# A speech joint network's gradients on one core: three loads and products moved in order, and another end of the program

## The chip, the cores and the metric

The kernel runs on one core of one Trainium2 chip. The core has five engines that each work through a list of instructions of their own: TensorE (PE, matrix products, with its weight loads PEld), VectorE (DVE), ScalarE (ACT), GpSimd (POOL) and SyncE (SP), which here only issues transfers. Transfers are issued by SP (which makes the hardware queue's requests) and by POOL (the software queue's), and run on the core's 16 DMA engines. An instruction whose input is not there holds up everything behind it in its engine's list. The metric is the time of one execution on the device in microseconds (us), lower is better; the time of a kernel is the median of its timed runs.

## The reference

The kernel computes a forward pass and all its gradients, in bfloat16. Cut to what matters:

```python
B, T, D, K, U = 2, 16000, 256, 3, 8
h  = gelu(conv(x, w1))[:, ::2]          # 3 taps, every second row kept: 8000 rows per batch
f  = gelu(conv(h, w2))[:, ::2]          # again: 4000 rows per batch
fe = f @ w_f;  ge = g @ w_g             # g: 8 prompts per batch, "bud,de->bue"
j  = tanh(fe[:, :, None, :] + ge[:, None, :, :])   # 2 x 4000 x 8 x 256
out = j @ w_o
# returned: out, and the gradients of x, w1, w2, g, w_f, w_g, w_o for a given grad_out
```

So the outputs are out_0 (the joint's product), out_1 (gradient of x), out_2 and out_3 (of w1 and w2, 3 x 256 x 256 each), out_4 (of the prompts g), out_5, out_6 and out_7 (of w_f, w_g and w_o, 256 x 256 each). The gradients of the weights are sums over all rows.

## The kernel before

The 2 x 4000 rows of the joint (with 16 empty ones between the batches) are one long line that is cut into G = 16 blocks of 512 columns; the last, block 15, has 336. The main loop over n does, in stage n, the joint of block n in four steps (`up` = 0 to 3, two prompts each) and, between its pieces, the convolutions of block n + 1 and the whole backward pass of block n - 1. `weave` mixes the two by a ratio written by hand. After the loop, the backward pass of block 15 stands alone.

**One step of the joint** (`joint_units`). `gj` (L653 to L667) multiplies the turned gradient GOT by w_o (L661, PE) and forms NGZ (L665, DVE); POOL adds the eight NGZ of a block up (L684) to NGFE. `o_block` makes out_0 (L710 on PE, L712 on ACT), which POOL stores (L737). `gwo` (L749) adds to w_o's gradient with rows JR of the tanh and rows GO of the gradient, one step later than they are loaded.

**Transfers.** SP issues, in one list, the turning loads of x (XC, L162) and of the gradient (GOT, L174), the plain loads of the gradient (GO, L204), the turning of the tanh into rows (JR, L691, in `load_jr`) and of F = gelu(conv) into rows (FR, L497, in `load_fr`, called when `up` is 1). POOL issues the stores of out_0 (L737) and of x's gradient (L257, in `store_gx`) and the loads of x rows for w1's gradient: XR (L215, in `load_xr`) and, for block 14, three early pieces (L246, in `load_xr_early`, called in steps 2 and 3 of stage 14) into three XC buffers, two pieces of 512 KB and one of 64 KB. Besides, POOL clears the tails of the short last block, among them FT's (L364, in `conv2_units`); FT has two buffers, so block 15's is free when block 13's has been read, and its last reader is the transfer FR of block 13.

**Backward pass of a block.** `d1_units` (L454, needs NGFE), `row_units` (turns rows on PE, L490, copied out at L492), `d5_units` (L477, L480), `gwf_units` (w_f's gradient, L535), `gw2_units` (w2's, L553), `ghr_units` (more rows), `e_units`: for each of 4 sets (3 in block 15) x's gradient (`gx_block`, L616 on PE, L619 on ACT, two GX buffers) and, for the first three, one tap of w1's gradient (`gw1`, L629). The sums over blocks are kept by `flush` (L438, DVE) in the fp32 tiles ACCF, ACC2 and ACC1.

**What sets the order.** The framework plans: it runs through the instructions with estimated times and gives each engine a list, in which an instruction that it takes to be ready can go ahead of others that were written earlier. Two means hold it back: `keep_in_program_order` (behind what was written before on the same engine) and `add_manual_dep` with NOSYNC (behind one named instruction of the same engine; an order, not a wait). `load_xr` has the first, `load_xr_early` and `load_fr` have none. `late` and `later` hold GELU pieces that `pump` hands out between matmuls.

**Start.** While the first x arrives, `warm` runs products of zeros on PE (L799): 12, then the prompts' transposes of `prompt_units` (L807, they need GR8, loaded by POOL), then 9, then the convolution of block 0 (L336). The prompts' second unit (L816, GE) follows it.

**End.** After the last backward pass each fp32 sum is copied to a bf16 tile and stored by SP (ACC1 on ACT, L915; ACC2 on DVE, L918; ACCF, L921; w_o's sum from PSUM, L924), and the prompts' gradients are formed: a sum over NGGEc (L928), and per batch a product with w_g turned (L937, out_4), transposes (L943, L945) and a product with the prompts (L947), at last L951 and the store of out_6 (L952).

Of the kernel before, what the change touches and what calls it, by code (L numbers as in the profile page):

```python
# [32 lines left out]
def kernel(  # L33
# [206 lines left out]
    def load_xr_early(n, piece):  # L240
# [5 lines left out]
        nc.gpsimd.dma_start(out=t[:, :(r1 - r0) * D], in_=x_rows(x, b, row + r0, P, r1 - r0, 4 * nsets(n)))  # L246
# [3 lines left out]
    def store_gx(n, k, t):  # L250
        s = nsets(n)
        for b, q, col, w in segs(n):
            p0, p1, row = col // s, (col + w) // s, 4 * (q + k) - 3
            if q + k == 0:
                nc.gpsimd.dma_start(out=out_1[b, 0:1, :], in_=t[p0:p0 + 1, 3, :])
                p0, row = p0 + 1, row + 4 * s
            nc.gpsimd.dma_start(out=x_rows(out_1, b, row, p1 - p0, 4, 4 * s),  # L257
                                in_=t[p0:p1].rearrange("p f d -> p (f d)"))
# [175 lines left out]
    def flush(key, acc, ps):  # L434
        if first_flush[key]:
            nc.vector.tensor_copy(out=acc, in_=ps)
        else:
            nc.vector.tensor_tensor(out=acc, in0=acc, in1=ps, op=ALU.add)  # L438
# [55 lines left out]
    def load_fr(n):  # L494
        W = geom(n)[1]
        FR = packed(frp.tile([P, KT, 4, P], BF16, name="FR")[:], "k a d", n, k=KT, d=P)
        nc.sync.dma_start_transpose(out=FR.rearrange("p k a d -> p (k a) d"),  # L497
                                    in_=S[n]["FT"].rearrange("p k w -> p (k w)"))
        S[n]["FR"] = FR
# [28 lines left out]
    def gwf_units(n):  # L528
# [9 lines left out]
        flush("F", ACCF[:], ps[:])  # L538
# [3 lines left out]
    def gw2_units(n):  # L542
        W = geom(n)[1]
        HG = S[n]["HG"]
        for i in (1, 2, 0):
# [10 lines left out]
            flush("2", ACC2[:, i, :], ps[:])  # L556
# [39 lines left out]
    def e_units(n):  # L596
# [26 lines left out]
        def gw1(i):  # L623
# [10 lines left out]
            flush("1", ACC1[:, i, :], ps[:])  # L634
# [209 lines left out]
    for _ in chain(warm(12), islice(prompts, 1), warm(9), conv_units(0), prompts, islice(conv1, 2), islice(turned, 3),  # L844
                   conv2_units(0)):
        pass
# [7 lines left out]
    for n in range(G):  # L854
# [16 lines left out]
        for up in range(U // 2):  # L871
# [5 lines left out]
            if up == 1:  # L877
# [30 lines left out]
    for _ in chain(d1_units(n), alternate(row_units(n), d5_units(n)), gwf_units(n), gw2_units(n), ghr_units(n), e_units(n)):  # L908
        pass


    fin = gel
    for i in range(KK):
        t_ = fin.tile([P, 512], BF16, name="g_sq", tag="g_sq")
        nc.scalar.copy(out=t_[:], in_=ACC1[:, i, :])  # L915
        nc.sync.dma_start(out=out_2[i].rearrange("(dt p) n -> p dt n", p=P), in_=t_[:].rearrange("p (k n) -> p k n", k=KT))
        t_ = fin.tile([P, 512], BF16, name="g_s", tag="g_s")
        nc.vector.tensor_copy(out=t_[:], in_=ACC2[:, i, :])  # L918
        nc.sync.dma_start(out=out_3[i].rearrange("(dt p) n -> p dt n", p=P), in_=t_[:].rearrange("p (k n) -> p k n", k=KT))
    t_ = fin.tile([P, 512], BF16, name="g_x", tag="g_x")  # L920
    nc.vector.tensor_scalar(out=t_[:], in0=ACCF[:], scalar1=-1.0, scalar2=None, op0=ALU.mult)  # L921
    nc.sync.dma_start(out=out_5.rearrange("(dt p) n -> p dt n", p=P), in_=t_[:].rearrange("p (k n) -> p k n", k=KT))
    t_ = fin.tile([P, 512], BF16, name="g_x", tag="g_x")
# [3 lines left out]
    NGGE = accp.tile([P, KT, CW], FP32, name="ACCN")[:, 0, :B * KT * U].rearrange("p (b k u) -> p b k u", b=B, k=KT)  # L927
    nc.vector.tensor_reduce(out=NGGE.rearrange("p b k u -> p (b k u)"),  # L928
                            in_=NGGEc[:].rearrange("p b k u c -> p (b k u) c"),
                            axis=mybir.AxisListType.X, op=ALU.add)  # L930
    NGGEb = ngzp.tile([P, KT, CW], BF16, name="NGZ")[:, 0, :B * KT * U].rearrange("p (b k u) -> p b k u", b=B, k=KT)
    nc.vector.tensor_copy(out=NGGEb, in_=NGGE)
    GWG_ps = ps_f32()
    for b in range(B):
        gg = ps_f32()
        for kt in range(KT):
            nc.tensor.matmul(gg[:U, 0:D], lhsT=NGGEb[:, b, kt, :], rhs=WGT[:, kt, :], start=(kt == 0), stop=(kt == KT - 1))  # L937
# [45 lines left out]
```

## Time and profile before

| | |
|---|---|
| median of 3 timed runs | 838.62 us (830.61 to 847.44) |
| the profiled execution | 823.52 us |
| its span, first to last instruction | 821.7 us |
| mean granted TensorE clock | 0.998 |
| PE busy | 794.8 us, 97% of the span |
| ACT, DVE, POOL busy | 679.0, 619.3, 401.2 us |
| PE busy in a typical 50 us (200 to 250) | 49.73 us |
| PE busy in the first 60 us | 47.47 us |
| DMA, mean | 230 GB/s, the 16 engines' share at 9 tenths or more up to the last two slices of 40 |

How to read it: busy time is the time an engine spent in its instructions; a matmul's end is modelled, so that PE's busy time can hide short gaps. In a timeline row the columns are the start, the length, the engine, the line, the operation, what it writes and reads, how many instructions are merged, and in brackets the idle time of that engine before it with what ended it. "SPq" rows are the queue's own: their length is the time until SP had handed the transfer over, which includes waiting. The profiled execution is shorter than each of the three timed runs; durations below come from it.

### The profile page before, as it was taken

The numbers are of one execution on the slowest core, as the hardware profiler recorded it, in microseconds if no ns is written. First come the engines' busy times: TensorE is split into PE (matmuls) and PEld (weight loads), VectorE is DVE, ScalarE is ACT, GpSimd is POOL, SyncE is SP. The second block draws the span as 40 slices with busy tenths as digits, with TensorE's granted clock in tenths as the row PEclk, the third lists the DMA queues.
The fourth block names the chain that finished last, engine by engine and source line by source line (L and its number), as shares of the span: only waits on it lengthen the run. The fifth ranks groups of instructions, "written<-read, shape, count | busy, mean of one in ns | idle before, by whom it ended". The sixth has DMA issues, their size and how long they took to land.

```text
span 821.7 us, 16450 instructions
## 1 busy us (share of the span) xinstructions
PE 794.8 (97%) x6234; PEld 592.1 (72%) x6309; DVE 619.3 (75%) x1193; ACT 679.0 (83%) x1080; POOL 401.2 (49%) x422
## 2 busy tenths in 40 slices
PE   8778999999999999999999999999999999999997
PEld 3445867867777776877868678677777768678796
DVE  4996786977869788687876869778697886868534
ACT  4999897996979879798897979969798797788644
POOL 1265554553554445454586544535544454455641
PEclk9999999999999999999999999999999999999999
DMA  9999999999999999999999999999999999999963
GB/s 223 210 203 233 231 250 254 246 273 218 243 247 220 265 236 201 241 291 218 245 230 251 218 238 244 246 217 253 248 233 231 250 251 154 225 223 267 254 146 92
DMA packets 401383, 189.38 MB, mean 230 GB/s; under 512 B 349304, under 2 KB 385056, under 8 KB 401304
## 3 DMA queue, kind: packets, MB, share of 16 engines
q1 hardware_dynamic: 380984, 121.21, 81.5%
q0 software_dynamic: 20320, 67.12, 26.8%
q8 instruction: 49, 0.80, 0.5%
q14 instruction: 30, 0.25, 0.1%
HBM read 51.39 MB, written 50.34 MB: 124 GB/s over the span
## 4 chain that ended last, share of the span: by engine, by line
PE 83%; ACT 6%; DVE 5%; DMA 3%; issue 3%; POOL 1%; POOLq 0%; DVEq 0%; ACTq 0%
PE GWO_ps L749 12%; PE ps L710 12%; PE ps L661 10%; PE ps L616 9%; PE ps L629 9%; PE ps L336 7%; PE pst L490 5%; PE ps L553 5%; PE ps L477 5%; PE ps L371 4%; ACT JT L424 2%; PE ps L535 2%; PE ps L454 1%; DMA JR<-JT 1%; ACT OUT L712 1%
## 5 line engine op out<-in xcount | busy, mean ns | idle before, releaser
L684 POOL TENSOR_TENSOR ACCN<-ACCN,NGZ 128x1024 f32<-128x1024 f32 (+1 forms) x80 | 169.5, 2118 | 74.6 <-DVE NGZ L665 73.5
L665 DVE SCALAR_TENSOR_TENSOR NGZ<-JSQ,ps 128x512 bf16<-128x512 bf16 (+3 forms) x272 | 168.4, 640 | 46.6 <-PE ps L661 34.6
L424 ACT ACTIVATE JT<-FE,GE 128x512 bf16<-128x512 f32 (+3 forms) x272 | 176.2, 711 | 0.5
L712 ACT CAST OUT<-ps 128x512 bf16<-128x512 f32 (+1 forms) x252 | 145.9, 595 | 36.3 <-PE ps L710 34.9
L653 ACT ACTIVATE JSQ<-JT 128x1024 bf16<-128x1024 bf16 (+1 forms) x128 | 134.8, 1059 | 35.8 <-DVE NGZ L665 35.6
L710 PE MATMUL ps<-WO,JT 128*128 128x256 bf16 (+1 forms) x1008 | 149.4, 272 | 4.9 <-DVE NGZ L665 3.8
L749 PE MATMUL GWO_ps<-GO,JR 128*128 128x256 bf16 (+1 forms) x1008 | 148.8, 273 | 2.8 <-DMA JR<-JT 2.1
L737 POOL DMA_DIRECT2D out_dram<-OUT x76 | 56.0, 738 | 165.2 <-ACT OUT L712 155.8
L661 PE MATMUL ps<-GOT,WOT 128*128 128x512 bf16 (+1 forms) x483 | 133.0, 374 | 2.4 <-ACT FE L397 0.9
L749 PEld LDWEIGHTS <-JR 128*128 128x128 bf16 (+1 forms) x1008 | 97.2, 98 | 29.7 <-DMA JR<-JT 3.6
L710 PEld LDWEIGHTS <-JT 128*128 128x128 bf16 (+1 forms) x1008 | 97.4, 98 | 26.3 <-issue 5.4
L616 PE MATMUL ps<-W1T,GH 128*128 128x256 bf16 (+2 forms) x756 | 100.4, 273 | 0.7
L616 PEld LDWEIGHTS <-GH 128*128 128x128 bf16 (+2 forms) x756 | 83.5, 116 | 13.0
L276 DVE SCALAR_TENSOR_TENSOR g_s<-g_sq,g_x 128x1024 bf16<-128x1024 bf16 (+2 forms) x35 | 67.9, 1940 | 30.3 <-ACT g_sq L276 30.3
L438 DVE TENSOR_TENSOR ACC<-ACC,ps 128x512 f32<-128x512 f32 x90 | 61.5, 684 | 36.9 <-PE ps L553 25.9
L336 PE MATMUL ps<-XC,W 128*128 128x512 bf16 (+1 forms) x359 | 85.2, 374 | 0.8
L629 PE MATMUL ps<-rows,XR 128*128 128x256 bf16 (+1 forms) x708 | 84.6, 273 | 0.0
L619 ACT CAST GX<-ps 128x512 bf16<-128x512 f32 (+2 forms) x126 | 72.4, 589 | 13.1 <-PE ps L616 5.8
L629 PEld LDWEIGHTS <-XR 128*128 128x128 bf16 (+1 forms) x708 | 69.3, 98 | 11.0
L257 POOL DMA_DIRECT2D out_dram<-GX x67 | 36.9, 551 | 81.2 <-ACT GX L619 79.4
L661 PEld LDWEIGHTS <-WOT 128*128 128x128 bf16 x512 | 48.2, 98 | 34.5 <-issue 3.5
L336 PEld LDWEIGHTS <-W 128*128 128x128 bf16 x384 | 37.5, 98 | 38.4 <-issue 0.4
(133 smaller groups left out, 1216.4 us busy)
## 6 DMA issues: line engine op xcount, KB each, us to landing
GO<-in_grad_out_dram SPq DMA_DIRECT2D x56, 512.0 KB, 5.5
out_dram<-OUT POOLq DMA_DIRECT2D x56, 512.0 KB, 5.9
out_dram<-GX POOLq DMA_DIRECT2D x55, 256.0 KB, 5.2
XR<-in_x_dram POOLq DMA_DIRECT2D x36, 256.0 KB, 9.3
XR<-in_x_dram POOLq DMA_DIRECT2D x12, 320.0 KB, 8.3
GO<-in_grad_out_dram SPq DMA_DIRECT2D x4, 384.0 KB, 5.0
out_dram<-OUT POOLq DMA_DIRECT2D x4, 384.0 KB, 5.0
GOT<-in_grad_out_dram SPq DMA_TRANSPOSE x68, 6.3
```

The lines of the kernel that those rows point to most:

```text
L336: nc.tensor.matmul(ps[:, :W], lhsT=W1[:, i, kt, mt * P:(mt + 1) * P], rhs=st["X", c][:, kt, 16 + sh:16 + sh + W], start=(k == 0), stop=(k ...
L424: act = nc.scalar.activation(out=JT[:, mt, lo:hi], in_=S[n]["FE"][:, mt, lo:hi], func=ACT.Tanh, bias=GE[:, b, mt, u:u + 1], scale=1.0)
L616: nc.tensor.matmul(ps[:M, cj * D:(cj + 1) * D], lhsT=GH[:, par, kt, o:o + s * (M - 1) + 1:s], rhs=W1T[:, i, kt, :], start=(j == 0), stop=( ...
L619: nc.scalar.copy(out=t[:M, 2 * cp:2 * cp + 2, :], in_=ps[:M, :])
L629: nc.tensor.matmul(ps[:, dt * D:(dt + 1) * D], lhsT=x_row(4 * k + i + 2 * (1 - par))[:M, dt * P:(dt + 1) * P], rhs=t[:M, g + 2 * par:g + 2 ...
L653: jsq = nc.scalar.activation(out=JSQ[:, :, :W], in_=JT[:, :, :W], func=ACT.Square)
L661: nc.tensor.matmul(ps[:, :W], lhsT=WOT[:, kt, mt * P:(mt + 1) * P], rhs=GOT[:, kt, :W], start=(kt == 0), stop=(kt == KT - 1))
L665: nc.vector.scalar_tensor_tensor(out=NGZ[:, mt, lo:hi], in0=JSQ[:, mt, lo:hi], scalar=1.0, in1=ps[:, lo:hi], op0=ALU.subtract, op1=ALU.mul ...
L684: st["last"] = nc.gpsimd.tensor_tensor(out=out, in0=in0, in1=st["NGZ", u][:, :, :W], op=ALU.add)
L710: nc.tensor.matmul(ps[:M, j * V:(j + 1) * V], lhsT=st["JT", u][:, kt, o:o + M], rhs=WO[:, kt, :], start=(kt == 0), stop=(kt == KT - 1))
L712: nc.scalar.copy(out=OUT[:M, k, :], in_=ps[:M, :])
L749: nc.tensor.matmul(GWO_ps[:, dt, :], lhsT=JR[:M, j, dt, k, :], rhs=GO[:M, k, j * V:(j + 1) * V], start=(n_gwo[0] == 0), stop=(n_gwo[0] == ...
```

## The change

The early x rows of block 14 are kept in program order on POOL. `load_fr` is called in step 3 of a stage instead of step 1, and from block 1 on the transfer stands behind the tanh rows JR of the block's last step. The two warm calls become one of 22, and both prompt units come behind the first convolution. In the last block `flush` writes the last sum straight into a bf16 tile (for w_f with the sign turned in the same instruction) and stores it; the prompts' gradients become a generator that alternates with w2's products; w_o's copy stands ahead of the last backward pass; and the last set's store of x's gradient is issued by SP.

```diff
@@ -243,7 +243,8 @@
         t = xcp.tile([P, 2, KT, CW + 16], BF16, name="XC")[:].rearrange("p c k w -> p (c k w)")
         (b, q, col, w), = segs(n)
         row = 4 * q - 3
-        nc.gpsimd.dma_start(out=t[:, :(r1 - r0) * D], in_=x_rows(x, b, row + r0, P, r1 - r0, 4 * nsets(n)))
+        tc.keep_in_program_order(nc.gpsimd.dma_start(out=t[:, :(r1 - r0) * D],
+                                                     in_=x_rows(x, b, row + r0, P, r1 - r0, 4 * nsets(n))))
         rows = t[:, :8 * D].rearrange("p (f d) -> p f d", f=8)
         S[n].setdefault("XRS", []).extend(rows[:, r] for r in range(r1 - r0))
 
@@ -254,8 +255,8 @@
             if q + k == 0:
                 nc.gpsimd.dma_start(out=out_1[b, 0:1, :], in_=t[p0:p0 + 1, 3, :])
                 p0, row = p0 + 1, row + 4 * s
-            nc.gpsimd.dma_start(out=x_rows(out_1, b, row, p1 - p0, 4, 4 * s),
-                                in_=t[p0:p1].rearrange("p f d -> p (f d)"))
+            queue = nc.sync if n == G - 1 and k == s - 1 else nc.gpsimd
+            queue.dma_start(out=x_rows(out_1, b, row, p1 - p0, 4, 4 * s), in_=t[p0:p1].rearrange("p f d -> p (f d)"))
             if q + w == MQ and k == 0:
                 nc.gpsimd.dma_start(out=out_1[b, T - 3:T, :].rearrange("(o f) d -> o f d", o=1), in_=t[p1:p1 + 1, 0:3, :])
 
@@ -431,8 +432,15 @@
 
     first_flush = {"1": True, "2": True, "F": True}
 
-    def flush(key, acc, ps):
-        if first_flush[key]:
+    def flush(key, acc, ps, to=None):
+        if to is not None:
+            o = gel.tile([P, 512], BF16, name="g_s", tag="g_s")
+            if key == "F":
+                nc.vector.scalar_tensor_tensor(out=o[:], in0=acc, scalar=-1.0, in1=ps, op0=ALU.mult, op1=ALU.subtract)
+            else:
+                nc.vector.tensor_tensor(out=o[:], in0=acc, in1=ps, op=ALU.add)
+            nc.sync.dma_start(out=to.rearrange("(dt p) n -> p dt n", p=P), in_=o[:].rearrange("p (k n) -> p k n", k=KT))
+        elif first_flush[key]:
             nc.vector.tensor_copy(out=acc, in_=ps)
         else:
             nc.vector.tensor_tensor(out=acc, in0=acc, in1=ps, op=ALU.add)
@@ -494,8 +502,10 @@
     def load_fr(n):
         W = geom(n)[1]
         FR = packed(frp.tile([P, KT, 4, P], BF16, name="FR")[:], "k a d", n, k=KT, d=P)
-        nc.sync.dma_start_transpose(out=FR.rearrange("p k a d -> p (k a) d"),
-                                    in_=S[n]["FT"].rearrange("p k w -> p (k w)"))
+        dma = nc.sync.dma_start_transpose(out=FR.rearrange("p k a d -> p (k a) d"),
+                                          in_=S[n]["FT"].rearrange("p k w -> p (k w)"))
+        if n:
+            tc.add_manual_dep(dma.ins, S[n]["JRD", 3].ins.name, NOSYNC, reason="rows of F behind tanh rows")
         S[n]["FR"] = FR
 
     def row_units(n):
@@ -535,7 +545,7 @@
                 nc.tensor.matmul(ps[:, dt * D:(dt + 1) * D], lhsT=FR[:M, dt, k, :],
                                  rhs=t[:M, 2 * k:2 * k + 2, :].rearrange("p k d -> p (k d)"),
                                  start=(k == 0 and dt == 0), stop=(k == len(bl) - 1 and dt == KT - 1))
-        flush("F", ACCF[:], ps[:])
+        flush("F", ACCF[:], ps[:], out_5 if n == G - 1 else None)
         first_flush["F"] = False
         yield
 
@@ -553,7 +563,7 @@
                     nc.tensor.matmul(ps[:, dt * D:(dt + 1) * D], lhsT=lhsT,
                                      rhs=HG[k][:M, 4:6, :].rearrange("p k d -> p (k d)"),
                                      start=(k == 0 and dt == 0), stop=(k == nsets(n) - 1 and dt == KT - 1))
-            flush("2", ACC2[:, i, :], ps[:])
+            flush("2", ACC2[:, i, :], ps[:], out_3[i] if n == G - 1 else None)
             yield
         first_flush["2"] = False
 
@@ -631,7 +641,7 @@
                                          rhs=t[:M, g + 2 * par:g + 2 * par + 2, :].rearrange("p k d -> p (k d)"),
                                          start=(j == 0 and dt == 0 and par == 0),
                                          stop=(j == len(bl) - 1 and dt == KT - 1 and par == 1))
-            flush("1", ACC1[:, i, :], ps[:])
+            flush("1", ACC1[:, i, :], ps[:], out_2[i] if n == G - 1 else None)
 
         for j, (k, M) in enumerate(bl):
             yield from gx_block(k, M)
@@ -841,7 +851,7 @@
     load_go(*orderp[0])
     load_got(*orderp[1])
     conv1, turned, prompts = conv_units(1), transposed_units(), prompt_units()
-    for _ in chain(warm(12), islice(prompts, 1), warm(9), conv_units(0), prompts, islice(conv1, 2), islice(turned, 3),
+    for _ in chain(warm(22), conv_units(0), prompts, islice(conv1, 2), islice(turned, 3),
                    conv2_units(0)):
         pass
     pump_late(len(late))
@@ -874,7 +884,7 @@
                 load_got(*orderp[step + 2])
             if step + 1 < len(orderp):
                 load_go(*orderp[step + 1])
-            if up == 1:
+            if up == 3:
                 load_fr(n)
             if back and up < 2 and n < G - 1:
                 load_xr(n - 1, 2 * up)
@@ -905,51 +915,45 @@
         gwo(*prev_gwo[0], k)
     for piece in range(4):
         load_xr(n, piece)
-    for _ in chain(d1_units(n), alternate(row_units(n), d5_units(n)), gwf_units(n), gw2_units(n), ghr_units(n), e_units(n)):
-        pass
-
-
-    fin = gel
-    for i in range(KK):
-        t_ = fin.tile([P, 512], BF16, name="g_sq", tag="g_sq")
-        nc.scalar.copy(out=t_[:], in_=ACC1[:, i, :])
-        nc.sync.dma_start(out=out_2[i].rearrange("(dt p) n -> p dt n", p=P), in_=t_[:].rearrange("p (k n) -> p k n", k=KT))
-        t_ = fin.tile([P, 512], BF16, name="g_s", tag="g_s")
-        nc.vector.tensor_copy(out=t_[:], in_=ACC2[:, i, :])
-        nc.sync.dma_start(out=out_3[i].rearrange("(dt p) n -> p dt n", p=P), in_=t_[:].rearrange("p (k n) -> p k n", k=KT))
-    t_ = fin.tile([P, 512], BF16, name="g_x", tag="g_x")
-    nc.vector.tensor_scalar(out=t_[:], in0=ACCF[:], scalar1=-1.0, scalar2=None, op0=ALU.mult)
-    nc.sync.dma_start(out=out_5.rearrange("(dt p) n -> p dt n", p=P), in_=t_[:].rearrange("p (k n) -> p k n", k=KT))
-    t_ = fin.tile([P, 512], BF16, name="g_x", tag="g_x")
+    t_ = gel.tile([P, 512], BF16, name="g_x", tag="g_x")
     nc.scalar.copy(out=t_[:], in_=GWO_ps[:].rearrange("p k v -> p (k v)"))
     nc.sync.dma_start(out=out_7.rearrange("(dt p) n -> p dt n", p=P), in_=t_[:].rearrange("p (k n) -> p k n", k=KT))
 
-    NGGE = accp.tile([P, KT, CW], FP32, name="ACCN")[:, 0, :B * KT * U].rearrange("p (b k u) -> p b k u", b=B, k=KT)
-    nc.vector.tensor_reduce(out=NGGE.rearrange("p b k u -> p (b k u)"),
-                            in_=NGGEc[:].rearrange("p b k u c -> p (b k u) c"),
-                            axis=mybir.AxisListType.X, op=ALU.add)
-    NGGEb = ngzp.tile([P, KT, CW], BF16, name="NGZ")[:, 0, :B * KT * U].rearrange("p (b k u) -> p b k u", b=B, k=KT)
-    nc.vector.tensor_copy(out=NGGEb, in_=NGGE)
-    GWG_ps = ps_f32()
-    for b in range(B):
-        gg = ps_f32()
-        for kt in range(KT):
-            nc.tensor.matmul(gg[:U, 0:D], lhsT=NGGEb[:, b, kt, :], rhs=WGT[:, kt, :], start=(kt == 0), stop=(kt == KT - 1))
-        gg_sb = rowp.tile([P, 8, P], BF16, name="rows")[:U, 0:2, :].rearrange("u a b -> u (a b)")
-        nc.scalar.activation(out=gg_sb, in_=gg[:U, 0:D], func=ACT.Copy, scale=-1.0)
-        nc.sync.dma_start(out=out_4[b], in_=gg_sb)
-        tr = ps_bf()
-        for kt in range(KT):
-            nc.tensor.transpose(out=tr[:U, kt, :], in_=NGGEb[:, b, kt, :], identity=ident[:])
-        ngR = rowp.tile([P, 8, P], BF16, name="rows")[:U, 0:KT, :]
-        nc.vector.tensor_copy(out=ngR, in_=tr[:U, 0:KT, :])
-        for dt in range(KT):
-            nc.tensor.matmul(GWG_ps[:, dt * D:(dt + 1) * D], lhsT=GRE[:, b, dt * P:(dt + 1) * P],
-                             rhs=ngR[:].rearrange("u kt p -> u (kt p)"),
-                             start=(b == 0 and dt == 0), stop=(b == B - 1 and dt == KT - 1))
-    t_ = fin.tile([P, 512], BF16, name="g_sq", tag="g_sq")
-    nc.scalar.activation(out=t_[:], in_=GWG_ps[:], func=ACT.Copy, scale=-1.0)
-    nc.sync.dma_start(out=out_6.rearrange("(dt p) n -> p dt n", p=P), in_=t_[:].rearrange("p (k n) -> p k n", k=KT))
+    def prompt_gradients():
+        NGGE = accp.tile([P, KT, CW], FP32, name="ACCN")[:, 0, :B * KT * U].rearrange("p (b k u) -> p b k u", b=B, k=KT)
+        nc.vector.tensor_reduce(out=NGGE.rearrange("p b k u -> p (b k u)"),
+                                in_=NGGEc[:].rearrange("p b k u c -> p (b k u) c"),
+                                axis=mybir.AxisListType.X, op=ALU.add)
+        NGGEb = ngzp.tile([P, KT, CW], BF16, name="NGZ")[:, 0, :B * KT * U].rearrange("p (b k u) -> p b k u", b=B, k=KT)
+        nc.vector.tensor_copy(out=NGGEb, in_=NGGE)
+        yield
+        gg, tr = ps_f32(), ps_bf()
+        for b in range(B):
+            for kt in range(KT):
+                nc.tensor.matmul(gg[:U, b * D:(b + 1) * D], lhsT=NGGEb[:, b, kt, :], rhs=WGT[:, kt, :],
+                                 start=(kt == 0), stop=(kt == KT - 1))
+            for kt in range(KT):
+                nc.tensor.transpose(out=tr[:U, b * KT + kt, :], in_=NGGEb[:, b, kt, :], identity=ident[:])
+        o = gel.tile([P, 512], BF16, name="g_sq", tag="g_sq")
+        nc.scalar.activation(out=o[:U], in_=gg[:U, 0:B * D], func=ACT.Copy, scale=-1.0)
+        nc.sync.dma_start(out=out_4.rearrange("b u d -> u b d"), in_=o[:U].rearrange("u (b d) -> u b d", b=B))
+        ngR = gel.tile([P, 512], BF16, name="g_sq", tag="g_sq")
+        nc.vector.tensor_copy(out=ngR[:U], in_=tr[:U, 0:B * KT, :].rearrange("u k p -> u (k p)"))
+        yield
+        ps = ps_f32()
+        for b in range(B):
+            for dt in range(KT):
+                nc.tensor.matmul(ps[:, dt * D:(dt + 1) * D], lhsT=GRE[:, b, dt * P:(dt + 1) * P],
+                                 rhs=ngR[:U, b * D:(b + 1) * D],
+                                 start=(b == 0 and dt == 0), stop=(b == B - 1 and dt == KT - 1))
+        o = gel.tile([P, 512], BF16, name="g_sq", tag="g_sq")
+        nc.scalar.activation(out=o[:], in_=ps[:], func=ACT.Copy, scale=-1.0)
+        nc.sync.dma_start(out=out_6.rearrange("(dt p) n -> p dt n", p=P), in_=o[:].rearrange("p (k n) -> p k n", k=KT))
+        yield
+
+    for _ in chain(d1_units(n), alternate(row_units(n), d5_units(n)), gwf_units(n),
+                   alternate(gw2_units(n), prompt_gradients()), ghr_units(n), e_units(n)):
+        pass
 
 
 # ---- launch: one core; inputs and outputs as the reference has them ----
```

## The prediction

> **What bounds the kernel now.** I read the page first: busy time by engine, then the chain that ended last.
>
> ```profile
> PE 794.8 (97%) x6234; PEld 592.1 (72%) x6309; DVE 619.3 (75%) x1193; ACT 679.0 (83%) x1080; POOL 401.2 (49%) x422
> ...
> PE 83%; ACT 6%; DVE 5%; DMA 3%; issue 3%; POOL 1%; POOLq 0%; DVEq 0%; ACTq 0%
> ```
>
> TensorE bounds it: of 821.7 us it leaves 26.9. The change adds and removes hardly any matmul, so it can only win from these. Busy times by stretch tell where they lie: in the first 60 us PE is busy 47.5 (12.5 lost); from 200 to 700, 50 us at a time, 49.7 (0.3 lost each, once 0.7); then
>
> ```profile
> 705.00:710.00 5.00, 4.95 (x44) 4.24 (x43) 4.93 (x12) 3.84 (x6) 2.59 (x5) 1.00 1.08 272
> 710.00:715.00 5.00, 4.04 (x28) 2.53 (x27) 3.49 (x5) 3.46 (x6) 4.80 (x4) 1.00 1.13 209
> 715.00:720.00 5.00, 4.12 (x27) 2.33 (x25) 2.08 (x5) 5.00 (x10) 2.96 (x4) 1.00 1.25 207
> ```
>
> (span, then busy PE, PEld, DVE, ACT, POOL, clock, DMA share, GB/s): 1.84 us lost, 1.7 more than the usual. From 760 to 765 it loses 1.02, and after its last large product, at 814.9, 6.8 us are left of the span. The rest is steady and out of reach.
>
> The timeline of the loss at 710, all engines:
>
> ```profile
> 688.10 10.91 SPq L174 DMA_TRANSPOSE GOT<-in_grad_out_dram  x1
> ...
> 700.91 2.70 SPq L497 DMA_TRANSPOSE FR<-FT  x1
> ...
> 704.33 3.62 SPq L691 DMA_TRANSPOSE JR<-JT  x1
> ...
> 705.74 0.23 POOL L364 MEMSET FT<- 128x96 bf16 x1 [10.29 <-issue]
> 706.26 0.55 POOL L257 DMA_DIRECT2D out_dram<-GX  x1 [0.29 <-ACT JT L424]
> ...
> 711.54 0.59 ACT L619 CAST GX<-ps 128x512 bf16<-128x512 f32 x1 [2.70 <-DMA out_dram<-GX]
> ...
> 712.18 1.02 PE L661 MATMUL ps<-GOT,WOT 128*128 128x512 bf16 x4 [0.83 <-ACT GX L619]
> ```
>
> POOL stands 10.29 us at L364: FT is not free until FR of block 13 has landed (issued 700.91, 4.4 median). Behind it stand GX's stores; ACT waits 2.70 for a GX buffer, PE 0.83 for ACT, and NGFE is late after that. FR was late because SP's list was: GOT took 10.91 where the same place a stage earlier took 3.24 (638.15). In just that time the first early load (POOL, issued 681.83, 512 KB) was under way, 16.1 us; from 680 to 690 the DMA engines moved 98 GB/s, a stage earlier (630 to 642) 307. That the load is the cause is my reading; the rate is low already from 680.0.
>
> **Part 1, early rows.** The first load, pinned behind block 14's store L737 of 737.42, goes to about 738, the others behind the store of 751.90. Issuing costs POOL 0.55 each: the pair fits in its idle 1.47 before L257 at 754.14; without that cover NGFE (760.39), for which PE already waits 0.97, is up to 1.1 later. The data are needed by w1's products at 784.3; 752.7 + 13.5 (median landing) = 766.2. Gain: SP's list at 690 to 704 is some 8 us earlier. The cost in stage 14 lies between 0 (the early load of 723.1, beside which PE was busy 19.88 of 720 to 740) and 8.6 (below). I take 0, by that row, the nearest. **Part 2, F's rows.** JR of each block's last step goes ahead of FR: by 1.24 to 3.07 us (FR's rows). JR of block 12 was issued at 646.24, landed 8.2 later and was used at 658.80: it has 4.4 us to spare, so the gain is 0 in this execution. FR's users have more: L535 of block 13 at 730.82, 25 us after landing; of block 15 at 803.29 against 784.4 + 2.5 + 1.2 + 4.4 = 792.5. For L364 it works against Part 1: 8 us earlier by the load, 3.6 (JR's 3.62) later by the order. Net 4.4 of the 10.29 us go, and I expect POOL's list, planned anew, to put L364 behind a store or an addition. What was late by at most 2.70 on ACT is then in time: **gain 1.7**, bounds 1.8 and, if L364 stays and FR is not earlier, a loss of 3.6. Next late is the loss at 760 (NGFE behind the 2.94 us clearing of XR), which stays.
>
> **Part 3, prompts.** The start:
>
> ```profile
> 1.82 5.18 PE L799 MATMUL ps<-rows 128*128 128x512 bf16 x12 [1.82 <-DVE rows L790]
> ...
> 7.93 0.25 PE L807 MATMUL pst<-ident,GX 8*128 8x8 bf16 x4 [0.93 <-DMA GX<-in_g_dram]
> 8.11 2.12 PE L799 MATMUL ps<-rows 128*128 128x512 bf16 x9
> ...
> 10.06 5.35 PE L336 MATMUL ps<-XC,W 128*128 128x512 bf16 x24
> ```
>
> Twelve warm products run at 0.427 us each (weight loads every 0.43), to 6.95; the next nine at (10.06 - 8.11)/9 = 0.217. Between them stands the wait for the prompts. Without it 22 end at 6.95 + 10 x 0.217 = 9.12, and the convolution starts 0.94 sooner. x is there: its second load was issued at about 2.2 and landed within 5.7, at 7.9; W1 at 1.3 + 5.0. Bounds: all 22 slow end at 11.2 (1.15 lost). The Trainium skill ("TensorE: Matmul & The Clock Gate", "What's actually happening") lets the clock rise after about 3.4 us of work, and says that the point varies by run; here the slow spacing still shows at 6.06, 4.2 us after the start, so the measurement decides. From 12.8 to 29 the chain runs through DVE, which takes on the copy gT, 0.17, that lay in its idle time; PE's wait for it is hidden, as PE waits for DVE there anyway (if not, 0.5). JR of step 0 follows the tanh, so all later moves along: **gain 0.94 - 0.2 = 0.7**.
>
> **Part 4, the end.** The chain, in order of time:
>
> ```profile
> 813.59 1.33 PE ps L629 x12
> 814.94 0.45 DVE ACC L438
> ...
> 817.13 0.39 PE ps L947 x2
> ...
> 817.59 0.60 ACT g_sq L951
> ```
>
> The last store was issued at 818.21 and took 1.8 to land. PE's list is full from 797 to 814.92 (6.00 of 6.00), so the prompts' products add to it there: 8 of 256 columns at 1.97/18 = 0.109 and 4 transposes at 0.06, 1.1 us, to 816.0. Then one flush of 0.69 to 816.7, no copy on ACT (0.62), and SP issues at 816.8: 818.21 - 816.8 = **1.4 sooner**. The last GX copy ends at 814.61 + 1.1 = 815.7; by SP, 0.4, and 1.8 to 3.0 to land (g_sq and g_x rows; POOL's 2.6): level with the last sum, so nothing more. The copies L915, L918, L921 (1.86, 1.08, 0.42) ran beside PE and give nothing; w_o's copy, 0.59, falls in ACT's idle 2.64 before 801.14. The sign in F's flush: 0.69, as the DVE rows of that form. Two waits are new. The prompts' last products wait for a copy on DVE (0 to 0.4). And the seven flushes share three g_s buffers: the fourth, w2's last at about 806.9, waits for F's store (804.9 + 0.4 + 2.1 = 807.4); behind it on DVE stand the row copies L492, for which PE's L629 waits. Bounds of the end: 0 and 1.5.
>
> **Sum.** 823.52 - 1.7 - 0.7 - 1.4 = 819.7, 3.8 us (0.46%) less. The three timed runs lie 7 to 24 above the profiled one, for a reason that the trace does not show; I take the same 3.8 from their median: 838.62 - 3.8 = **834.8**. Two per cent (16.8 us), about what three runs with this scatter tell from no change, is four times the forecast.
>
> **Rivals.** *A, slower: the early loads slow the end of stage 14.* GOT beside the first load landed 15.8 after issue instead of 6.3 (9.5 late), x 19.1 instead of 6.1 (13.0). In stage 14, JR of the last step (issued 752.27, 7.3 to land, used 765.76) has 6.2 to spare, GOT of step 1 (758.57 + 6.3, used 769.31) 4.4. Lateness beyond 4.4 is PE's; at 13.0 it is 8.6, more than the 3.8 won: 834.8 + 8.6 = 843.4. It turns to slower than before at 8.2 of lateness. For it: two loads of 512 KB, not one, 14 us apart. Against: the load of 723.1 cost PE nothing, and stage 14 turns no x (two transfers of 2.8). By the Trainium skill ("DMA: Bandwidth & Descriptors", "Queues, rings and completion order") an engine takes turns between its queues packet by packet; that would share the rate and not cut it to 98 GB/s, so by the rule alone, 512 KB at 290 GB/s, 1.8 us late, this rival would be nothing. Chance 0.15. *B, slower: the new order doesn't free POOL.* L364 stays where it was and FR, behind JR, is no earlier: POOL stands 3.6 longer, PE loses 3.6 instead of winning 1.7: 834.8 + 5.3 = 840.1. Chance 0.15. *C, faster by 2%:* what the timed runs have above the profile, 15.1 us, is JR coming too late at 14 boundaries (1.08 each, its 4.4 used up by a slower DMA); FR's place gives back 1.24 or more each, so all of it: 819.7. Nothing in the trace shows such waits after 68 us. Chance 0.08. *D, the clock rises sooner:* with 8 slow products (0.427) and 14 quick ones (0.217) the 22 end at 1.82 + 3.42 + 3.04 = 8.3, 0.8 sooner than in the sum: 834.0. Against it: the eleven slow spacings of the trace. The Trainium skill's 3.4 us, above, would be these 8 products. Chance 0.05. The forecast keeps 0.57.
>
> **Numbers.** Faster by over 2%: 0.09 (C, and scatter); slower by over 2%: 0.07 (A with more lateness, and scatter); within: 0.84. The range leaves out C and the upper edge of A: the runs' own scatter (-8.0, +8.8) about 834.8 is 826.8 to 843.6; widened by the unknown costs, 822 to 848.
>
> **What would show it.** Right: L364 with a short wait, PE 4.9 of 5 in 710 to 720's place; no L246 before stage 14's second store; L336 first at 9.1; JR ahead of FR at each boundary; the last SP issue 1.4 nearer to the last L629. Wrong: PE waiting for GOT or JR from 755 to 780, DVE waiting before its fourth g_s, slow spacing up to the 22nd warm product.

## The result, and the profile after

The changed kernel took 837.44 us, the median of 6 executions (829.5 to 855.1); the kernel before, beside it, 828.74 (824.61 to 847.44). The ratio is **1.0104, with a 95% interval of 1.0065 to 1.0143**: slower by 1.0%. (All ratios here leave out executions more than 1.5% above the fastest of their kernel, up to 7 of 12 where a kernel's times scatter most, so that there the median, which is over all executions, says more.) The forecast was 834.8 and 0.46% faster. The time lies within the 822 to 848 that was stated, but these are some 13 us to either side of a base, 838.62 from three executions, that was high: the 35 executions of the kernel before in the last comparison below have a median of 827.33. What counts is the ratio, and its sign was wrong.

The profiled execution of the changed kernel took 835.12 us, its span is 833.1, 11.4 longer than before's 821.7. The lines of the source have moved: FT's clearing is L365 (before L364), the stores of GX L259 (L257), the GX copies L629 (L619), NGFE L694 (L684), FR L505 (L497), JR L701 (L691), `gj`'s product L671 (L661), the large last products L639 (L629).

The page, busy time by engine and the chain that ended last:

```profile
PE 803.1 (96%) x6310; PEld 594.0 (71%) x6310; DVE 615.7 (74%) x1188; ACT 677.6 (81%) x1076; POOL 404.1 (48%) x421
...
PE 79%; ACT 7%; DMA 6%; DVE 3%; issue 2%; POOL 2%; SPq 0%; POOLq 0%; DVEq 0%; ACTq 0%
```

DMA has 6% of the chain instead of 3%. PE is busy 8.3 us longer, with no more work to speak of: some matmuls ran slower. Where, the stretches tell that answer to before's 705 to 720 (span, then busy PE, PEld, DVE, ACT, POOL, clock, DMA share, GB/s):

```profile
710.00:715.00 5.00, 5.00 (x44) 4.24 (x43) 4.93 (x12) 2.96 (x5) 0.00 (x0) 1.00 1.04 196
715.00:720.00 5.00, 1.31 (x12) 1.02 (x11) 0.01 (x1) 0.00 (x0) 2.86 (x5) 0.85 1.10 230
720.00:725.00 5.00, 0.50 (x2) 0.22 (x2) 0.00 (x0) 1.14 (x3) 3.40 (x2) 0.50 1.15 298
725.00:730.00 5.00, 5.00 (x20) 2.35 (x19) 2.08 (x6) 5.00 (x10) 1.42 (x3) 0.62 1.02 246
```

PE loses 8.2 us between 715 and 725, where before it lost 1.84 in all. Then it is "busy" for 5.00 us with 20 matmuls, where 44 fit from 710 to 715: the granted clock was 0.50 and 0.62. Three rows of the view of waits (us in total, times, longest) are one chain:

```profile
POOL FT L365 <- DMA FR<-FT: 15.0, 1, 15.0
...
ACT GX L629 <- DMA out_dram<-GX: 11.5, 2, 10.9
...
PE ps L671 <- ACT GX L629: 8.2, 1, 8.2
```

The timeline shows them in order:

```profile
699.85 0.56 POOL L259 DMA_DIRECT2D out_dram<-GX  x1
...
707.52 3.47 SPq L701 DMA_TRANSPOSE JR<-JT  x1
...
711.08 1.26 SPq L505 DMA_TRANSPOSE FR<-FT  x1
...
715.43 0.18 POOL L365 MEMSET FT<- 128x96 bf16 x1 [15.03 <-DMA FR<-FT]
715.96 0.54 POOL L259 DMA_DIRECT2D out_dram<-GX  x1 [0.35 <-issue]
...
723.86 0.58 ACT L629 CAST GX<-ps 128x512 bf16<-128x512 f32 x1 [10.90 <-DMA out_dram<-GX]
724.50 1.87 PE L671 MATMUL ps<-GOT,WOT 128*128 128x512 bf16 x4 [8.19 <-ACT GX L629]
```

FR of block 13 stands directly behind JR, as the change has it. The clearing stands in POOL's list where it stood before, with GX's store behind it, and waits 15.03 us for FR instead of 10.29. The store is issued at 715.96, and 7.8 later, by the chain that ended last, it sets ACT free; PE goes on when ACT has made its copy. Four matmuls that take 1.02 elsewhere take 1.87 after the stall.

The starts of NGFE, one per stage, show what this is of the 11.4 (after less before): +1.1 up to stage 7; up to stage 8 another 3.75 (from 423 to 453 the DMA engines moved 133 to 172 GB/s, before's 231 to 257; PE waits 1.8 there for XR rows, and the clock is 0.83 over the last ten us); then nothing until stage 12; from there to stage 14 **7.9** (4.8 and 3.1); stages 14 to 15 are equal, 31.52 in both; the end is 1.36 shorter. 1.1 + 3.75 + 7.9 - 1.36 = 11.4.

### The profile page after: what moved, and what is told of

It is laid out like the page before. It is cut to its first block, busy times and chain, and to the rows that moved or that the text cites. A ratio compares the mean times of both kernels' runs of the same rounds, so it can differ in the third digit from the quotient of the medians.

```text
span 833.1 us, 16510 instructions
## 1 busy us (share of the span) xinstructions
PE 803.1 (96%) x6310; PEld 594.0 (71%) x6310; DVE 615.7 (74%) x1188; ACT 677.6 (81%) x1076; POOL 404.1 (48%) x421
## 4 chain that ended last, share of the span: by engine, by line
PE 79%; ACT 7%; DMA 6%; DVE 3%; issue 2%; POOL 2%; SPq 0%; POOLq 0%; DVEq 0%; ACTq 0%
PE GWO_ps L759 11%; PE ps L720 11%; PE ps L671 10%; PE ps L639 9%; PE ps L626 9%; PE ps L337 7%; PE pst L498 5%; PE ps L563 5%; PE ps L485 4%; PE ps L372 4%; ACT JT L425 2%; DMA XR<-in_x_dram 2%; PE ps L545 2%; PE ps L462 1%; PE ps L396 1%
## 5 line engine op out<-in xcount | busy, mean ns | idle before, releaser
L694 POOL TENSOR_TENSOR ACCN<-ACCN,NGZ 128x1024 f32<-128x1024 f32 (+1 forms) x80 | 169.3, 2117 | 75.0 <-DVE NGZ L675 73.5
L671 PE MATMUL ps<-GOT,WOT 128*128 128x512 bf16 (+1 forms) x512 | 139.6, 377 | 8.5 <-ACT GX L629 8.2
L629 ACT CAST GX<-ps 128x512 bf16<-128x512 f32 (+2 forms) x126 | 72.4, 588 | 21.1 <-DMA out_dram<-GX 11.5
L337 PE MATMUL ps<-XC,W 128*128 128x512 bf16 (+1 forms) x360 | 87.3, 380 | 0.6 <-DMA XC<-in_x_dram 0.6
L639 PE MATMUL ps<-rows,XR 128*128 128x256 bf16 (+1 forms) x708 | 85.1, 273 | 1.8 <-DMA XR<-in_x_dram 1.8
L446 DVE TENSOR_TENSOR ACC<-ACC,ps 128x512 f32<-128x512 f32 x84 | 57.4, 684 | 35.0 <-PE ps L563 26.1
L639 PEld LDWEIGHTS <-XR 128*128 128x128 bf16 (+1 forms) x708 | 69.1, 98 | 13.3 <-DMA XR<-in_x_dram 2.3
L671 PEld LDWEIGHTS <-WOT 128*128 128x128 bf16 x512 | 48.4, 98 | 41.5 <-issue 10.1
L259 POOL DMA_DIRECT2D out_dram<-GX x66 | 36.3, 550 | 85.3 <-ACT GX L629 80.8
```

The source lines that it names most:

```text
L337: nc.tensor.matmul(ps[:, :W], lhsT=W1[:, i, kt, mt * P:(mt + 1) * P], rhs=st["X", c][:, kt, 16 + sh:16 + sh + W], start=(k == 0), stop=(k ...
L629: nc.scalar.copy(out=t[:M, 2 * cp:2 * cp + 2, :], in_=ps[:M, :])
L639: nc.tensor.matmul(ps[:, dt * D:(dt + 1) * D], lhsT=x_row(4 * k + i + 2 * (1 - par))[:M, dt * P:(dt + 1) * P], rhs=t[:M, g + 2 * par:g + 2 ...
L671: nc.tensor.matmul(ps[:, :W], lhsT=WOT[:, kt, mt * P:(mt + 1) * P], rhs=GOT[:, kt, :W], start=(kt == 0), stop=(kt == KT - 1))
L694: st["last"] = nc.gpsimd.tensor_tensor(out=out, in0=in0, in1=st["NGZ", u][:, :, :W], op=ALU.add)
```

## The experiments

**Theory 1:** the loss is Part 2, at one place: FR of block 13, put behind JR, makes the clearing of FT hold POOL's list longer, and the stores of GX behind it hold ACT and PE. **Theory 2:** the new order of transfers, or the early loads of Part 1, costs something at every boundary. **Rival A** of the prediction: the early loads slow stage 14.

### Part 2 alone, and the change without it

```diff
 # F's rows alone: before, with
+        if n:
+            tc.add_manual_dep(dma.ins, S[n]["JRD", 3].ins.name, NOSYNC, ...)
-            if up == 1:
+            if up == 3:
                 load_fr(n)
 # without F's rows: the changed kernel, with these lines as they were before
```

> The kernel before with part 2 alone (F's rows called in step 3 and ordered behind the tanh rows). Theory 1, POOL's clearing of FT waits for F's rows, which now come last: POOL stands about 15 us at the clearing, PE loses 6 to 10 us there, the time is 0.7 to 1.2% above before. Rival, the early x rows or the DMA engines' rate cause the loss: no difference to before, wait at the clearing about as before (10 us or less).

> The changed kernel with part 2 taken back. Theory 1: the loss at the boundary of stages 13 and 14 falls from some 8 us to 2 or less, the time is 0 to 0.5% below before (the end's 1.4 us are left). Rival, early rows or the rate of the DMA engines: still 0.7 to 1.2% above before.

Part 2 alone: 847.75 us (823.86 to 853.5, 4 executions; too scattered for a ratio), the kernel before beside it 831.48. Of its profile (853.5 us) the boundary of stages 13 and 14 is read first; the view of waits:

```profile
POOL FT L364 <- DMA FR<-FT: 22.2, 1, 22.2
...
PE ps L663 <- ACT GX L621: 13.4, 1, 13.4
```

PE's wait is longer than the 6 to 10 us expected. The change without Part 2: 824.11 (819.18 to 848.15, 10), ratio 0.9987 (0.9925 to 1.0049). Its clearing waits 0.56, and PE is busy 19.84 of the 20 us from 700 on. So the loss comes with Part 2 and goes with it. That leaves open whether the clearing is the way.

### The clearing moved, the transfers untouched

```diff
 # in conv2_units: into the changed kernel, into before, into before with Part 2
-            nc.gpsimd.memset(FT[:, :, W:], 0.0)
+            tc.keep_in_program_order(nc.gpsimd.memset(FT[:, :, W:], 0.0))
```

In the changed kernel only POOL's list differs: the clearing stands behind the three stores of GX, three of out_0, the XR loads and the additions that it used to hold up, and comes after block 13's NGFE. FR stays behind JR for every block.

> The changed kernel with one edit: the clearing of FT's tail is kept in program order on POOL, so that it stands some 15 us later in POOL's list; all other lists are the same. Theory 1: no wait at the clearing, POOL's idle 15 us gone, PE loses under 1 us at that boundary, 0.2 to 0.6% below before. Rival: nothing changes, 0.7 to 1.2% above before.

> The kernel before with one edit: the clearing of FT's tail kept in program order on POOL. Theory: with F's rows in their old place the wait at the clearing is 0.6 to 10 us by the execution (0.56, 4.7 and 10.29 in three profiles) and costs PE 0 to 1.8, so the median falls by 0 to 0.2% and the scatter stays (median near before's, runs up to 850).

> The kernel before with part 2 and the clearing in program order. Theory 1: the loss of part 2 alone is gone, since nothing of it was in F's rows themselves; at most as long as before. Second theory, F's rows behind the tanh rows do help executions with a slow transfer rate (rival C of the prediction): fewer waits of PE for tanh rows, runs scatter less than those with F's rows in the old place, median 0.3 to 1% below before. Rival, they do nothing: median and scatter as for the edit of the clearing alone.

The changed kernel with it: **821.23** (819.55 to 828.03, 10), ratio **0.9951 (0.9909 to 0.9993)**. Its stretches over the same boundary:

```profile
700.00:720.00 20.00, 19.84 (x153) 15.38 (x155) 17.75 (x34) 18.89 (x34) 10.67 (x11) 1.00 1.19 239
720.00:740.00 20.00, 19.89 (x179) 15.47 (x180) 13.94 (x27) 15.57 (x26) 8.74 (x15) 1.00 1.14 197
```

Nothing is lost and the clock stays at 1.00, though FR was handed over at 706.59 to 709.68, behind JR, so as late as in a stalled execution. Part 2 alone with it: 825.32 (821.12 to 849.62, 10), 0.998 (0.9933 to 1.0027), instead of 847.75. The kernel before with it: 823.86 (821.98 to 838.54, 10), 0.9994 (0.9947 to 1.004). The kernel before beside these two had 827.26. Theory 2 falls for FR: with the late transfers in place and the clearing out of their way no loss is left at this boundary. Nor is there the gain that the second theory of the run with Part 2 expected: 0.3 to 1% less and less scatter did not come.

### One transfer of fifteen

Two kernels move FR of block 13 alone, two rows in SP's list; the lists of PE, ACT and POOL are the same as in the kernel that each starts from.

```diff
 # all but block 13: the changed kernel, with
-        if n:
+        if n and n != G - 3:
             tc.add_manual_dep(dma.ins, S[n]["JRD", 3].ins.name, NOSYNC, ...)
-            if up == 3:
+            if up == (1 if n == G - 3 else 3):
 # block 13 only: before, with
+        (n == G - 3) and tc.add_manual_dep(dma.ins, S[n]["JRD", 3].ins.name, NOSYNC, ...)
-            if up == 1:
+            if up == (3 if n == G - 3 else 1):
```

> The changed kernel with the transfer FR of block 13 alone in its old place, two rows earlier in SP's list and ahead of the tanh rows of the block's last step; FR of all other blocks stays behind them. POOL's, ACT's and PE's lists are the same as the changed kernel's. Theory 1 (the loss is one wait: the clearing of FT for block 15 behind FR of block 13): the clearing waits under 2 us, PE busy 19.8 of 20 at the boundary from stage 13 to 14, and the time is that of the pinned kernel, about 0.995 of before. Theory 2 (FR late at every boundary loses a little everywhere, through SP's list): the time stays near the changed kernel's, about 1.010 of before, and the pinned kernel's gain has another reason.

> The kernel before with the transfer FR of block 13 alone moved two rows later in SP's list, behind the tanh rows of the block's last step; all other lists are the same as before. Theory 1: this one row carries the loss: the clearing waits 15 us or more, PE waits 8 or more for ACT's GX buffer there, and the time is about 1.01 to 1.02 of before. Theory 2: one row of fifteen carries a fifteenth of the loss, within 0.2 per cent of before.

> The changed kernel once more, timed beside the three others. Theory 1: a wait of 15 us at the clearing again and 1.007 to 1.014 of before. If the first comparison was chance: 1.000, with a clearing that waits as briefly as in the kernel before.

> The changed kernel with the clearing of FT kept in program order, once more, timed beside the three others. Theory 1: no wait at the clearing, about 0.995 of before, below the changed kernel by 1.2 to 2 per cent. If its first comparison was chance: 1.000 of before, and level with the changed kernel.

| kernel, timed together | median us (lowest to highest) | ratio to before |
|---|---|---|
| before (35 executions) | 827.33 (819.99 to 860.99) | |
| changed, again (12) | 831.07 (822.24 to 846.09) | 1.0043 (0.9995 to 1.0092) |
| before, FR of block 13 moved (12) | 840.89 (823.5 to 857.75) | 1.0047 (0.9985 to 1.0108) |
| changed, FR of block 13 moved back (12) | 822.48 (819.57 to 830.34) | 0.9961 (0.9918 to 1.0004) |
| changed, clearing moved, again (12) | 824.05 (819.24 to 834.2) | 0.9945 (0.9901 to 0.9989) |

The changed kernel's loss is smaller this time, 1.0043 where 1.007 to 1.014 was expected, and its interval touches 1; the single row gave 1.0047 instead of 1.01 to 1.02. These two are the slowest all the same. The single row puts the stall into the kernel before; FR is about as late as in the changed kernel, and that the wait agrees to the hundredth of a us is chance (its timeline at this place):

```profile
708.43 3.48 SPq L691 DMA_TRANSPOSE JR<-JT  x1
712.00 1.26 SPq L497 DMA_TRANSPOSE FR<-FT  x1
...
715.58 0.18 POOL L364 MEMSET FT<- 128x96 bf16 x1 [15.03 <-DMA FR<-FT]
...
723.75 0.59 ACT L619 CAST GX<-ps 128x512 bf16<-128x512 f32 x1 [10.63 <-DMA out_dram<-GX]
724.38 1.86 PE L661 MATMUL ps<-GOT,WOT 128*128 128x512 bf16 x4 [7.93 <-ACT GX L619]
```

Further on this profile (850.69 us) loses more: PE waits 7.35 us at 764.32 for XR rows that took some 25 us to land, and 3.28 at 802.02 for ACT. The profile of Part 2 alone has the same two waits, 5.23 and 3.35; before's has neither, and its XR rows landed within 11.5. Whether the stall brings them about is not shown, so the medians 840.89 and 847.75 are not the price of the stall alone.

The same row moved back takes the stall out of the changed kernel, with FR of the other blocks still late:

```profile
691.11 1.67 SPq L505 DMA_TRANSPOSE FR<-FT  x1
693.49 3.45 SPq L701 DMA_TRANSPOSE JR<-JT  x1
695.52 0.20 POOL L365 MEMSET FT<- 128x96 bf16 x1
```

Theory 1 is shown for the stall, from both sides: moving the row makes it, and moving the row back or the clearing away removes it. The changed kernel's second profile (829.11 us) has the stall in a small form, a wait of 9.82 us instead of the 15 expected:

```profile
704.03 1.26 SPq L505 DMA_TRANSPOSE FR<-FT  x1
708.41 0.18 POOL L365 MEMSET FT<- 128x96 bf16 x1 [9.82 <-DMA FR<-FT]
...
715.24 0.59 ACT L629 CAST GX<-ps 128x512 bf16<-128x512 f32 x1 [4.10 <-DMA out_dram<-GX]
715.88 1.02 PE L671 MATMUL ps<-GOT,WOT 128*128 128x512 bf16 x4 [1.39 <-ACT GX L629]
```

**The price of the wait.** Put side by side, the profiles in which the clearing stands at its old place give a rule. "FR" is when SP had handed FR over, counted from the start of block 12's NGFE; "step" is from that NGFE to block 13's, 49.75 to 49.77 in all six profiles with the clearing moved:

| kernel | FR | wait of the clearing | step | over 49.77 |
|---|---|---|---|---|
| row moved back | 33.6 | 0 | 49.77 | 0 |
| without Part 2 | 34.5 | 0.56 | 49.77 | 0 |
| Part 4 alone | 37.2 | 4.75 | 49.77 | 0 |
| changed, again | 43.0 | 9.82 | 52.08 | 2.3 |
| before | 44.5 | 10.29 | 52.58 | 2.8 |
| changed | 48.4 | 15.03 | 57.37 | 7.6 |
| row moved alone | 49.0 | 15.03 | 57.30 | 7.5 |
| Part 2 alone | 56.4 | 22.20 | 64.46 | 14.7 |

The wait grows one for one with FR's lateness, to within 1 us. A wait of up to about 7.5 us is covered, that is, it costs nothing, and **all of it beyond 7.5 us goes into the step**: 10.29 - 7.5 = 2.8, 15.03 - 7.5 = 7.5, 22.20 - 7.5 = 14.7. (The 7.5 is fitted to these rows.) In the profiled run of the changed kernel the next step lost 3.1 more than before's, by the sum the rest of PE's stall and the low clock behind it. Part 2 sets FR behind GO and JR: 1.12 + 3.47 and the gaps, 4.8 us later in the changed kernel's list. The rest of FR's lateness is SP's list itself, which differs from one execution to the next: JR of that step was handed over 37.0 to 55.0 us after block 12's NGFE in the 14 profiles of the study. In the four profiles of the table with FR of block 13 ahead of JR the wait was beyond 7.5 once, in before; in the four with it behind JR, each time.

### The end, the start and the early rows

```diff
 # the end alone: before, with the change's hunks in store_gx, flush, the calls of flush and the program's end
 # clearing moved, without Part 3:
-    for _ in chain(warm(22), conv_units(0), prompts, ...
+    for _ in chain(warm(12), islice(prompts, 1), warm(9), conv_units(0), prompts, ...
 # clearing moved, without Part 1, in load_xr_early:
-        tc.keep_in_program_order(nc.gpsimd.dma_start(out=t[:, :(r1 - r0) * D], ...))
+        nc.gpsimd.dma_start(out=t[:, :(r1 - r0) * D], ...)
```

> The kernel before with part 4 alone (the other end). Theory 1: from the end of the last product of w1's gradient to the end of the span 1.4 us less net of the 1.1 us of products added ahead of it; 0.1 to 0.3% below before, hardly told from no change. Rival, the prompts' products delay the last block: no gain or up to 1 us loss.

> The changed kernel with the clearing in program order and part 3 taken back (warm products and prompts as before). Theory: part 3 starts the first convolution 1.9 us sooner but PE then waits 0.6 for x and 1.6 for the prompts' copy, and stage 0 waits for transfers, so it gives 0 to 0.7 us: ratio to before 0.994 to 0.997. Rival, part 3 gives its 1.5 us to the end: 0.2% more than with it.

> The changed kernel with the clearing in program order and part 1 taken back (early x rows where the planner puts them). Theory: the early rows cost or give nothing that can be measured, ratio to before 0.993 to 0.999 as with them (0.9951). Rival A of the prediction, early rows loaded in stage 14 delay the tanh rows of its last step: without them the waits of PE for tanh rows between stages 14 and 15 (3.6 us in one profile) go, 0.3 to 0.5% less.

The end alone: 832.97 (820.05 to 845.79, 10), ratio 1.0001 (0.9929 to 1.0072). The changed kernel with the clearing moved, without Part 3: 826.52 (820.39 to 859.42, 10), 0.9995 (0.994 to 1.0049); without Part 1: 822.8 (820.47 to 835.62, 10), 0.9987 (0.9942 to 1.0031). All three intervals hold 1 and overlap with that of the whole, 0.9951: what each part gives is below what these runs can tell (without Part 3, 0.994 to 0.997 was expected). The kernel before beside the last two had 827.26, beside the end alone 831.48. The profiles can tell it for two:

- **Part 4.** From block 15's NGFE to the end of the span, the five profiles without it took 29.5 to 29.8 us, eight of the nine with it 28.4 to 28.5 (the ninth, 31.0, has a wait of 2.4 for JR in that stretch). It wins 1.0 to 1.4.
- **Part 3.** Block 1's NGFE started at 114.2 on average of seven profiles without it (110.9 to 115.8) and at 113.0 of seven with it (111.0 to 115.1). A gain near 1 is likely; the scatter is larger.
- **Part 1.** JR of block 13's last step was handed over 45.3 us after block 12's NGFE on average of the seven profiles without it (37.0 to 55.0) and 43.4 of the seven with it (37.7 to 51.4). A gain of 8 us for SP's list is not there; 1.9 lies within the scatter.

Not run: Parts 1 and 3 each alone in the kernel before, and a third FT buffer, for which there was no room in memory.

## Why the prediction was wrong

**What bounds it, right.** PE, with the loss at 710 as the largest to be had, and POOL's wait at the clearing as its cause: all later runs bear that out, and pinning the clearing in the kernel before takes it away.

**Part 2 and the clearing, wrong; this is the step that failed.** The sum had "8 us earlier by the load, 3.6 (JR's 3.62) later by the order", and by it "Net 4.4 of the 10.29 us go". The second term was a little small, 4.8, as GO stands between as well. The first was wrong: with the early load gone SP's list was no earlier. The last XC ahead of FR and JR was handed over 42.2 us after block 12's NGFE instead of 41.7, and JR, which had FR's 2.70 no longer ahead of it, 1.8 earlier (48.8 to 47.0), not 8. The term rested on one coincidence, a load under way while the DMA engines moved 98 GB/s. The prediction itself noted that the rate was low before the load was issued, and yet put the whole excess of GOT, 10.91 over 3.24, into the sum. The changed kernel has the same dip without the load: from 674 to 685 its DMA engines moved 93 GB/s, and the GOT of that time is as slow, 76 us ahead of the first L246:

```profile
674.55 10.48 SPq L174 DMA_TRANSPOSE GOT<-in_grad_out_dram  x1
...
704.19 2.02 SPq L162 DMA_TRANSPOSE XC<-in_x_dram  x1
```

FR was handed over 3.9 later in all and took 1.0 longer to land, so that the wait grew by 4.7 instead of shrinking.

**"I expect POOL's list, planned anew, to put L364 behind a store or an addition"** did not happen: the clearing kept its place. This was the other leg that the gain of 1.7 stood on. An order that decides the sign should have been bounded, not expected: the text had the bound ("if L364 stays and FR is not earlier, a loss of 3.6") and gave it 0.15.

**Rival B was the mechanism that came true**, with the place and the way foretold, and its size short. It had POOL 3.6 longer and PE 3.6 slower, "834.8 + 5.3". Measured: POOL 4.7 longer, the step 4.8, and 3.1 more in the next. The one-for-one price that it used is right, since before's wait of 10.29 was already past the cover of 7.5. What it left out is PE's clock: after 8.19 us of idling the granted clock was 0.50 for some 4 us. The Trainium skill ("TensorE: Matmul & The Clock Gate", "What's actually happening") has the array at half rate after an idle window of about 3.4 us; the trace agrees: 1.87 us for four matmuls after 8.19 idle, 1.02 after the 1.39 of the second profile. Other waits place the step: after 2.42 us (for JR at 804.35, changed, again) the clock stayed at 1.00, after 3.55 (for JR at 777.46, changed, clearing moved) it was 0.50 for some 3 us. But short waits close together do it too: in the changed kernel's profile 0.65 and 1.17, at 446.78 and 448.55, were followed by 0.50 from 449 to 452. So a stall has a step in its price that no sum of waits shows.

**Part 1's cost, right in this profile.** No load early in stage 13, the first at 750.72, the others at 765.19, each behind its store; stage 14 to 15 took 31.52 us in both kernels. Rival A did not occur here. In the first profile with the clearing moved (828.03 us), which has the early loads at 738.02 and 752.49, its sign is there: PE waits 3.55 us for JR at 777.46, and this step took 36.91. With Part 1 taken back it took 31.52, but the median was no lower (822.8 beside 821.23), and the second profile with the clearing moved has the loads and 31.51 (the one without Part 3 has 34.19). So rival A is neither shown nor excluded for single executions.

**Part 3, right in kind.** The convolution started at 8.20, not 9.12:

```profile
1.82 6.54 PE L809 MATMUL ps<-rows 128*128 128x512 bf16 x22 [1.82 <-DVE rows L800]
8.20 1.03 PE L337 MATMUL ps<-XC,W 128*128 128x512 bf16 x4
9.84 4.48 PE L337 MATMUL ps<-XC,W 128*128 128x512 bf16 x20 [0.61 <-DMA XC<-in_x_dram]
```

That is rival D, almost to its 8.3, to which the prediction gave 0.05: fewer than 12 of the 22 ran slow. In other profiles the 22 took 6.31 to 7.86, so the point moves by execution, which the Trainium skill's same section says of it. x is the next limit, as the 0.61 shows. The profile's 1.45 gained here, read at block 0's NGFE, were lost again by block 1's and 1.28 more, beside waits of 0.85 for NGFE and 1.43 for JR up to 66.5 and a clock of 0.50 from 67 to 70; on average over the profiles about 1 us stays, less than the scatter.

**Part 4, right.** The last rows of the timeline:

```profile
827.75 1.48 PE L639 MATMUL ps<-rows,XR 113*128 113x256 bf16 x12
...
829.26 0.69 DVE L441 TENSOR_TENSOR g_s<-ACC,ps 128x512 bf16<-128x512 f32 x1 [1.94 <-PE ps L639]
829.98 0.37 SPq L442 DMA_DIRECT2D out_dram<-g_s  x1
```

SP issues its last store 0.75 after the last product instead of 3.3, and the span ends 3.9 after it instead of 6.8. Of these 2.9 PE gives 1.5 back, as it reaches its last product that much later after block 15's NGFE with the prompts' products ahead of it (forecast 1.1); 1.36 remain, forecast 1.4. The new waits on DVE were small (0.35 before w2's last flush).

**The sum.** Without the stall the change gives about what it was said to give: the forecast's ratio was 834.8 / 838.62 = 0.9954, and the changed kernel with the clearing moved measured 0.9951 and 0.9945, each with an interval of 0.4% to either side. That the figures agree so closely is luck and no proof of the terms: the 1.7 came from another order than the one forecast, and the clearing moved in the kernel before gave 0.9994.

**A version that beats both:** the changed kernel with the clearing in program order, 821.23 and 824.05 us beside 831.48 and 827.33 for the kernel before.

## What to carry to other kernels

An instruction of 0.18 us that waits on a transfer is as dangerous as what stands behind it in its engine's list: before a transfer is put later, find every instruction that waits for it, on every engine, and read how much of that wait is already past its cover; from there on each us was paid in full here. A cause read from one coincidence in one execution, such as a load beside a slow stretch of the DMA engines, should enter a sum only with zero as one of its ends. And where the sign hangs on how a planner will arrange a list, pin the order, or give both arrangements like chances.

## What the runs showed of the hardware

The DMA engines' rate dips for 10 to 30 us at places that change with the execution: 98 GB/s at 680 to 690 in before's profile, 93 at 674 to 685 in the changed kernel's; 133 to 172 at 423 to 453 in the latter, beside the 3.75 us lost there. No part of the change is seen to place them, and what triggers them stays open. The two slow GOT transfers (10.91 and 10.48 us) lie in such a dip or right behind it, and SP's list is late after them. How late it is differs by execution (37 to 55 us for the same transfer), and that decides whether a wait downstream is covered.

The stall had a tail: after PE resumed at 724.5 its clock was granted at 0.50 for about 4 us before it rose (0.81 from 728 to 730, 1.00 from 730), which makes some 2 us on top of the 8.19 (an estimate: 4 us of work at half rate).
